# Attention and cosine router: state in four quarters of the array, narrow matmuls on column tiles, counts by a scan, and a new order on each engine

## Chip, cores, metric

The kernel runs on one core of one Trainium2 chip. The metric is the device time of one execution in microseconds (us), median of several runs. All arithmetic is fp32.

## What is computed

An attention block with a decaying state (RWKV-5 form) feeds a top-1 router with eight experts. Cut to what matters:

```python
B, H, S, D = 4, 8, 768, 48            # attention
for t in range(S):
    cur = einsum('bhd,bhe->bhde', u * k_t, v_t)
    y[t] = einsum('bhd,bhde->bhe', r_t, state + cur)
    state = w * state + einsum('bhd,bhe->bhde', k_t, v_t)
x = y as (B*S, H*D) = (3072, 384)     # router, E = 8 experts, F = 1024
logits = unit(x) @ unit(expert_emb).T / tau
e = argmax(logits); gate = softmax(logits)[e]
out = gate * (relu(x @ w1[e]) @ w2[e])
```

The kernel cuts the 768 steps into six chunks of C = 128. One **unit** is one chunk of one batch, for all eight heads, so there are 24 units, and the four units of one chunk are a **group**. Inside a chunk the scores between the 128 steps are a masked 128 x 128 matrix (`AT`), and what is older comes from the state. Heads are treated in NP = 4 pairs; a pair's 48-wide heads lie at partitions 0 to 47 and 64 to 111 (DP = 64, PP = 112).

## The kernel before

One unit's work goes through these functions (`own_rows`, `carry` and `logits` stand, as they were, in the removed lines of the diff further down). `mm` and `nc.tensor` are TensorE (PE), `nc.vector` is VectorE (DVE), `nc.scalar` is ScalarE (ACT), `nc.gpsimd` is GpSimd (POOL). The PSUM buffers (`k.ps`) are single, but for the tags "tp" and "at", which have two buffers each and are handed out in turn: `rt`, `kt` and `yrows` take "tp" one after the other.

```python
def turn(k, i):
    nc = k.nc
    R, Kw = k.loaded[i][1], k.Kpad[i % len(k.Kpad)]
    rt = k.ps.tile([128, NP, C], F32, name="rt", tag="tp")
    for p in range(NP):
        nc.tensor.transpose(rt[:, p, :], pair(R, p), k.ident)
    RT = k.work.tile([128, NP, C], F32, name="RT", tag="RT")
    nc.vector.tensor_mul(RT, rt, k.rpow)
    kt = k.ps.tile([128, NP, C], F32, name="kt", tag="tp")
    for p in range(NP):
        nc.tensor.transpose(kt[:, p, :], pair(Kw, p), k.ident)
    KT = k.work.tile([128, NP, C], F32, name="KT", tag="KT")
    nc.scalar.copy(KT, kt)
    k.RT[i], k.KT[i] = RT, KT

def scores(k, i):
    nc = k.nc
    RT, KT = k.RT[i], k.KT.pop(i)
    at = [k.ps.tile([128, NP, C], F32, name="at", tag="at") for _ in range(2)]
    for p in range(NP):
        for s in range(2):
            rows = slice(s * DP, s * DP + D)
            nc.tensor.matmul(at[s][:, p, :], KT[rows, p, :], RT[rows, p, :], start=True, stop=True)
    k.AT[i] = []
    for s in range(2):
        a = k.work.tile([128, NP, C], F32, name=f"AT{s}", tag=f"AT{s}")
        nc.vector.tensor_mul(a, at[s], k.umask[:, None, :].to_broadcast([128, NP, C]))
        k.AT[i].append(a)

def states(k, i):
    nc = k.nc
    c, b = divmod(i, B)
    if c == NCH - 1:
        return
    V, Kw = k.loaded[i][2], k.Kpad[i % len(k.Kpad)]
    st = k.ps.tile([128, NP, 2 * D], F32, name="st", tag="st")
    for p in range(NP):
        nc.tensor.matmul(st[0:PP, p, :], pair(Kw, p)[:, 0:PP], pair(V, p), start=True, stop=True)
    k.st[i] = st

def sums(k, i):
    nc = k.nc
    mm = nc.tensor.matmul
    c, b = divmod(i, B)
    V, RT, AT, T = k.loaded[i][2], k.RT.pop(i), k.AT.pop(i), k.state[b]
    y = k.ps.tile([128, NP, C], F32, name="y", tag="y")
    if c > 0:
        for p in range(NP):
            mm(y[0:PP, p, :], T[:, p, 0:PP], RT[:, p, :], start=(p == 0), stop=False, skip_group_check=True)
    for p in range(NP):
        for s in range(2):
            mm(
                y[s * DP : s * DP + D, p, :], V[:, 2 * p + s, :], AT[s][:, p, :],
                start=(c == 0 and p == 0), stop=True, skip_group_check=True,
            )
    yT = k.yT[i % len(k.yT)]
    if c > 0:
        nc.scalar.copy(yT[0:PP], y[0:PP])
    else:
        for s in range(2):
            heads = slice(s * DP, s * DP + D)
            nc.scalar.copy(yT[heads], y[heads])
    if b == 0:
        k.groups[c] = group(k, c)

def rows(k, i):
    nc = k.nc
    c, b = divmod(i, B)
    yT = k.yT[i % len(k.yT)]
    y = k.ps.tile([128, NP, 2, DP], F32, name="yrows", tag="tp")
    for p in range(NP):
        nc.tensor.transpose(
            y[:, p].rearrange("q s d -> q (s d)")[:, 0:PP], yT[0:PP, p, :], k.ident[0:PP, 0:PP]
        )
    X = k.groups[c].X[:, b, :].rearrange("q (p s d) -> q p s d", p=NP, s=2)
    nc.vector.tensor_add(X, y[:, :, :, 0:D], k.xd.pop(i).rearrange("q (p s) d -> q p s d", s=2))
    del k.loaded[i]

def turn_rows(k, g, b):
    nc = k.nc
    X = g.X[:, b, :]
    xp = k.ps.tile([128, NK, C], F32, name="xp", tag="xp")
    for m in range(NK):
        nc.tensor.transpose(xp[:, m, :], X[:, m * 128 : (m + 1) * 128], k.ident)
    g.xT[b] = k.work.tile([128, NK, C], F32, name="xT", tag="xT")
    nc.scalar.copy(g.xT[b], xp)

def ranks(k, g):
    mm = k.nc.tensor.matmul
    g.rank = k.ps.tile([128, B, E], F32, name="rank", tag="st")
    mm(g.rank, k.umask, g.oh, start=True, stop=False)
    for b in range(1, B):
        mm(g.rank[:, b:B, :], k.ones, g.oh[:, 0 : B - b, :], start=False, stop=False, skip_group_check=True)
    mm(g.rank, k.ones, k.cum[:, None, :].to_broadcast([128, B, E]), start=False, stop=True)

def taken(k, g):
    g.take = k.ps.tile([QS, 128], F32, name="take", tag="st")
    for b in range(B):
        k.nc.tensor.matmul(
            g.take, g.what[:, b].rearrange("p q s -> p (q s)"), g.lane[:, b, :], start=(b == 0), stop=(b == B - 1)
        )
```

The loop below issues the instructions in program order, and each engine runs its own in that order. `on(f, i)` calls f for unit i, `of_group` the same for a unit of an earlier group object, and `whole(f, i)` calls f for the group whose last unit is i, once in four rounds. Functions such as `choose` (the arg-max over the logits, six small DVE instructions), `gates` (softmax of the chosen expert), `places` (position of each token in its expert's list) and `listed` (one-hot rows for `taken`) work on one group.

```python
def attention(k):
    units = B * NCH
    def on(f, i):
        if 0 <= i < units:
            f(k, i)
    def of_group(f, i):
        if 0 <= i < units:
            f(k, k.groups[i // B], i % B)
    def whole(f, i):
        if 0 <= i < units and i % B == B - 1:
            f(k, k.groups[i // B])
    emb = build_experts(k)
    for i in range(-1, units + 7):
        j = i - SETTLED * B
        if 0 < i + AHEAD < units:
            load(k, i + AHEAD)
        if i < 2:
            next(emb)
        whole(summed, i - 6)
        whole(places, i - 4)
        on(own_rows, i)
        on(turn, i + 1)
        on(scaled, i + 2)
        on(own, i + 1)
        on(states, i)
        of_group(squares, i - 1)
        whole(choose, i - 3)
        whole(listed, i - 5)
        if j == 10:
            k.lists = turned_lists(k, perm, "st")
            lists = taken_by_rank(k, k.lists)
            first = [Early(k, r, *lists, w) for r, w in zip(LAST, k.weights)]
        on(sums, i)
        on(carry, i)
        on(scores, i + 1)
        on(rows, i)
        of_group(put, i)
        on(own_sum, i + 1)
        of_group(turn_rows, i - 1)
        of_group(logits, i - 2)
        whole(ranks, i - 3)
        whole(gates, i - 3)
        if i == units:
            first[0].hidden(0)
        whole(taken, i - 5)
        # ... (cut) j == 7, 8, 9, 10: after four chunks, the experts are ordered by load, and
        # two experts' weights and first token tiles are fetched
        if i == units + 1:
            first[0].hidden(1)
        if i == units + 2:
            first[0].rows(0)
        if i == units + 4:
            first[0].rows(1)
            # ... (cut) counts, out(to)
            first[1].hidden(0)
    # ... (cut) final order, gathers; then the eight expert blocks
```

`first[...]` are two "early" experts, whose work (`early_h`, `early_y`) fills TensorE while the last lists are made. After the loop, eight expert blocks follow; the change does not touch them.

Of the kernel before, what the change touches and what calls it, by code (L numbers as in the profile page):

```python
# [10 lines left out]
F32 = mybir.dt.float32  # L11
# [9 lines left out]
C = 128  # L21
NCH = S // C
DP = 64
# [89 lines left out]
def build_consts(k):  # L113
# [21 lines left out]
    k.yT = [k.aconst.tile([128, NP, C], F32, name=f"yT{i}") for i in range(2)]  # L135
    for t in k.yT:
        nc.gpsimd.memset(t, 0.0)
    for b in range(B):
        t = k.aconst.tile([128, NP, 2 * DP], F32, name=f"state{b}")
        nc.gpsimd.memset(t, 0.0)  # L140
        k.state.append(t)
# [9 lines left out]
    k.qt = numbers(k, "qt", [QS, QS], [[TM, 2], [0, E], [1, TM]], 0, 0)  # L151
    k.turned = numbers(k, "turned", [QS, QS], [[0, 2], [1, E], [0, TM]], 1, 0)
    k.part = pool.tile([QS, 1], I32, name="part")
# [9 lines left out]
    k.sums = pool.tile([QS, 128], F32, name="sums")  # L163
    nc.gpsimd.memset(k.sums, 0.0)

    k.cum = pool.tile([128, E], F32, name="cum")


def build_turned(k):
# [4 lines left out]
    bits = pool.tile([QS, 3], I32, name="bits")  # L174
    nc.vector.tensor_scalar(bits[:, 0:1], k.part, 2, E - 1, ALU.arith_shift_right, ALU.bitwise_and)
    nc.vector.tensor_scalar(bits[:, 1:2], k.part, 3, None, ALU.bitwise_and)
    nc.vector.tensor_scalar(bits[:, 2:3], k.part, 5, 2, ALU.arith_shift_right, ALU.arith_shift_left)
    own = pool.tile([QS, 3], F32, name="own")
    nc.vector.tensor_copy(own, bits)
    nc.vector.tensor_add(own[:, 1:2], own[:, 1:2], own[:, 2:3])  # L180
    k.mask = pool.tile([QS, E], F32, name="mask")
    nc.vector.tensor_scalar(k.mask, k.number[0:QS], own[:, 0:1], None, ALU.is_equal)
# [26 lines left out]
def build_experts(k):  # L209
# [16 lines left out]
    k.ent = k.const.tile([128, NK, E], F32, name="ent")  # L226
    nc.vector.tensor_copy(k.ent, ps)
# [74 lines left out]
def own_rows(k, i):  # L302
    xd = k.work.tile([128, H, D], F32, name="xd", tag="xd")
    diag, V = k.diag.pop(i), k.loaded[i][2]
    for h in range(H):
        k.nc.scalar.mul(xd[:, h, :], V[:, h, :], diag[:, h : h + 1])  # L306
    k.xd[i] = xd


def turn(k, i):  # L310

    nc = k.nc
    R, Kw = k.loaded[i][1], k.Kpad[i % len(k.Kpad)]
# [3 lines left out]
    RT = k.work.tile([128, NP, C], F32, name="RT", tag="RT")  # L317
    nc.vector.tensor_mul(RT, rt, k.rpow)
# [3 lines left out]
    KT = k.work.tile([128, NP, C], F32, name="KT", tag="KT")  # L322
    nc.scalar.copy(KT, kt)  # L323
    k.RT[i], k.KT[i] = RT, KT

# [16 lines left out]
# [4 lines that stand above are left out]
    if c == NCH - 1:  # L346
        return
    V, Kw = k.loaded[i][2], k.Kpad[i % len(k.Kpad)]
    st = k.ps.tile([128, NP, 2 * D], F32, name="st", tag="st")
    for p in range(NP):  # L350
        nc.tensor.matmul(st[0:PP, p, :], pair(Kw, p)[:, 0:PP], pair(V, p), start=True, stop=True)
    k.st[i] = st


def carry(k, i):
# [5 lines left out]
    for s in range(2):  # L361
        rows = slice(s * DP, s * DP + D)
        part = T[rows, :, s * DP : s * DP + D]
        nc.vector.tensor_add(part, part, st[rows, :, s * D : (s + 1) * D])  # L364
    for s in range(2):
        rows = slice(s * DP, s * DP + D)
        part = T[rows, :, s * DP : s * DP + D]
        nc.gpsimd.tensor_mul(part, part, k.wC[rows])  # L368


def sums(k, i):

# [5 lines left out]
    y = k.ps.tile([128, NP, C], F32, name="y", tag="y")  # L378
    if c > 0:
        for p in range(NP):  # L380
            mm(y[0:PP, p, :], T[:, p, 0:PP], RT[:, p, :], start=(p == 0), stop=False, skip_group_check=True)
    for p in range(NP):
        for s in range(2):
            mm(  # L384
                y[s * DP : s * DP + D, p, :], V[:, 2 * p + s, :], AT[s][:, p, :],
                start=(c == 0 and p == 0), stop=True, skip_group_check=True,
            )
    yT = k.yT[i % len(k.yT)]
    if c > 0:
        nc.scalar.copy(yT[0:PP], y[0:PP])  # L390
    else:
        for s in range(2):
# [1023 lines left out]
```

## Time and profile before

The time is 457.1 us (median of 3 runs, 456.83 to 458.7). The profiled execution spans 458.0 us.

| stretch of the profiled execution | us | PE busy | DVE busy | ACT busy | POOL busy |
|---|---|---|---|---|---|
| start up to the `at` of unit 4 | 38.11 | 31.71 | 20.92 | 18.60 | 25.95 |
| units of chunk 1 | 27.07 | 26.30 | 17.97 | 16.90 | 19.16 |
| units of chunk 2 | 27.69 | 27.36 | 18.18 | 15.97 | 19.98 |
| units of chunk 3 | 27.68 | 27.35 | 17.83 | 15.97 | 18.36 |
| units of chunk 4 | 27.68 | 27.35 | 17.82 | 15.97 | 18.34 |
| chunk 5 up to the `at` of the last unit | 19.50 | 18.27 | 14.30 | 11.63 | 9.82 |
| last unit and lists, up to the first expert block | 40.62 | 38.26 | 14.19 | 8.19 | 12.92 |
| expert blocks to the end | 249.65 | 233.28 | 135.90 | 70.83 | 53.87 |

Each row is one window of the trace; an edge between rows is the start of the `at` matmuls of a unit (38.11, 65.18, 92.87, 120.55, 148.23 and 167.73 us after the span's start), and the last one is 208.35 us, the first transpose of the first expert block. Busy is the time in which the engine had an instruction running. Matmuls are pipelined, so a busy PE need not be one that works at its peak: one fp32 matmul is recorded as two instructions of some 270 ns each, while the next one may start 109 ns later. A transpose is one such record.

Lines such as L334 are lines of the kernel before; a line of the timeline gives start, duration, engine, line, operation, what is written and what is read, the number of instructions merged into it, and in brackets how long the engine had been idle and what released it.

### The profile page before, as it was taken

The page shows a single profiled execution, that of the slowest core. Times are in us where ns is not written, and L with a number is a line of the kernel's source. Part 1 is how long each engine was busy: PE and PEld are TensorE (multiplying, and loading weights), DVE is VectorE, ACT ScalarE, POOL GpSimd, SP SyncE. Part 2 cuts the span into 40 slices and gives each one's busy share as a digit, 9 for nine tenths or more (in the row PEclk, how much of TensorE's full clock was granted, in tenths as well). Part 3 has the DMA queues.
Part 4 walks back from the last instruction along what each step waited for, and adds up shares of the span by engine and source line. Part 5 has one row for each costly group of instructions (what it writes and reads, how often), then busy time and mean ns, then how long its engine had stood idle before and what let it go on. Part 6 is the DMA issues. An engine that isn't in the chain of part 4 may idle for free. (4 is left out here: it accounts for less than half of the span.)

```text
span 458.0 us, 8806 instructions
## 1 busy us (share of the span) xinstructions
PE 429.9 (94%) x3266; PEld 391.2 (85%) x3266; DVE 257.1 (56%) x611; ACT 174.0 (38%) x497; POOL 178.4 (39%) x260
## 2 busy tenths in 40 slices
PE   8879999999999998999999999999999999999970
PEld 3668989889888888777899999999999999899660
DVE  4556865765756773325676685715726636565310
ACT  2377646656556643113233323323323224132110
POOL 7765676685675732144004114113113113200310
PEclk9999999999999997999999999999999999999995
DMA  8766546546453188022435362433443351040110
GB/s 176 153 140 141 114 94 140 122 89 138 99 111 87 36 309 330 0 69 88 140 140 183 122 211 69 148 109 127 140 162 90 147 173 53 34 156 1 51 39 20
DMA packets 93799, 54.36 MB, mean 119 GB/s; under 512 B 76937, under 2 KB 88380, under 8 KB 93746
## 3 DMA queue, kind: packets, MB, share of 16 engines
q1 hardware_dynamic: 89024, 43.85, 34.7%
q0 software_dynamic: 3296, 9.44, 6.2%
q8 instruction: 28, 0.46, 0.4%
q10 hardware_dynamic: 1426, 0.41, 0.4%
q14 instruction: 25, 0.20, 0.1%
HBM read 44.45 MB, written 9.63 MB: 118 GB/s over the span
## 5 line engine op out<-in xcount | busy, mean ns | idle before, releaser
L1157 POOL DMA_INDIRECT out_dram<-y,to x25 | 30.5, 1220 | 179.7 <-issue 91.8
L1033 PE MATMUL ps<-xTe,w 128*128 128x192 f32 (+3 forms) x336 | 62.9, 327 | 0.0
L1033 PEld LDWEIGHTS ps<-xTe,w 128*128 128x128 f32 x336 | 55.9, 190 | 0.5
L306 ACT ACTIVATE xd<-V,diag 128x48 f32<-128x48 f32 x192 | 45.8, 321 | 19.3 <-DVE diag L298 14.9
L338 DVE TENSOR_TENSOR AT<-at,umask 128x512 f32<-128x512 f32 x48 | 30.9, 686 | 34.2 <-PE at L334 34.2
L1040 ACT ACTIVATE hT<-hT 128x384 f32<-128x384 f32 (+3 forms) x42 | 22.0, 523 | 33.8 <-DVE hT L1063 21.1
L1097 PE MATMUL ps<-Tw,Sh 128*128 128x192 f32 x192 | 32.5, 326 | 0.0
L334 PE MATMUL at<-RT,KT 48*128 48x128 f32 x384 | 27.9, 285 | 4.4 <-ACT KT L323 3.4
L1097 PEld LDWEIGHTS ps<-Tw,Sh 128*128 128x128 f32 x192 | 31.4, 190 | 0.0
L368 POOL TENSOR_TENSOR state<-state,wpow 48x192 f32<-48x192 f32 x40 | 20.4, 510 | 28.2 <-DVE state L364 26.7
L334 PEld LDWEIGHTS at<-RT,KT 48*128 48x128 f32 x384 | 23.3, 187 | 9.3 <-ACT KT L323 5.1
L899 POOL DMA_INDIRECT G<-xs,take x25 | 26.4, 1056 | 9.0 <-issue 5.2
L1033 PE MATMUL ps<-Tx,Sw 128*128 128x192 f32 (+3 forms) x168 | 29.7, 326 | 0.0
L1033 PEld LDWEIGHTS ps<-Tx,Sw 128*128 128x128 f32 x168 | 27.6, 190 | 0.1
L384 PE MATMUL y<-AT,V 128*48 128x128 f32 x384 | 25.9, 277 | 0.0
L1050 DVE TENSOR_TENSOR u<-ps,p 128x384 f32<-128x384 f32 (+3 forms) x14 | 7.8, 557 | 31.7 <-PE ps L1033 30.9
L292 POOL TENSOR_TENSOR KU<-KU,Rpad 128x384 f32<-128x384 f32 x24 | 24.0, 1001 | 1.9
L283 POOL TENSOR_TENSOR Kpad<-K,kpow 128x384 f32<-128x384 f32 x23 | 23.0, 1000 | 3.0 <-DVE kpow L101 1.8
L291 POOL TENSOR_TENSOR KU<-K,u_bc 128x384 f32<-128x384 f32 x24 | 24.0, 1000 | 0.3 <-DVE diag L298 0.3
L490 ACT COPY xT<-xp 128x384 f32<-128x384 f32 x24 | 11.5, 479 | 31.8 <-PE xp L488 31.8
L1097 PE MATMUL ps<-w,hT 128*128 128x192 f32 x128 | 23.4, 326 | 0.0
L384 PEld LDWEIGHTS y<-AT,V 128*48 128x48 f32 x384 | 19.8, 122 | 3.0
(234 smaller groups left out, 903.1 us busy)
## 6 DMA issues: line engine op xcount, KB each, us to landing
w<-in_moe_w_dram SPq DMA_DIRECT2D x16, 1536.0 KB, 6.6
K<-in_k_dram SPq DMA_DIRECT2D x24, 192.0 KB, 3.5
V<-in_v_dram SPq DMA_DIRECT2D x24, 192.0 KB, 3.6
xs<-X SPq DMA_DIRECT2D x24, 192.0 KB, 2.0
Rpad<-in_r_dram SPq DMA_DIRECT2D x23, 192.0 KB, 3.8
G<-xs,take POOLq DMA_INDIRECT x27
out_dram<-y,to POOLq DMA_INDIRECT x25
Rpad<-in_r_dram ACTq DMA_DIRECT2D x1, 192.0 KB, 3.9
```

The source lines that it names most:

```text
L283: k.nc.gpsimd.tensor_mul(k.Kpad[i % len(k.Kpad)][:, :, 0:D], k.loaded[i][0], k.kpow)
L291: nc.gpsimd.tensor_mul(KU, K, k.u_bc)
L292: nc.gpsimd.tensor_mul(KU, KU, R[:, :, 0:D])
L306: k.nc.scalar.mul(xd[:, h, :], V[:, h, :], diag[:, h : h + 1])
L334: nc.tensor.matmul(at[s][:, p, :], KT[rows, p, :], RT[rows, p, :], start=True, stop=True)
L338: nc.vector.tensor_mul(a, at[s], k.umask[:, None, :].to_broadcast([128, NP, C]))
L384: mm(y[s * DP : s * DP + D, p, :], V[:, 2 * p + s, :], AT[s][:, p, :], start=(c == 0 and p == 0), stop=True, skip_group_check=True,)
L899: nc.gpsimd.indirect_dma_start(out=G[0:n, :], out_offset=None, in_=k.xs[:, :], in_offset=IndirectOffsetOnAxis(ap=take[0:n], axis=0), bound ...
L1033: nc.tensor.matmul(ps[:, j, :], weights[:, (f + j) * 128 : (f + j + 1) * 128], moving, start=(first and j == 0), stop=True, skip_group_che ...
L1040: nc.scalar.activation(h, h, ACT.Relu)
L1097: nc.tensor.matmul(ps, a[:, f, :], b[:, f, :], start=(first and f == 0), stop=(f == NF // 2 - 1), skip_group_check=True)
L1157: k.nc.gpsimd.indirect_dma_start(out=k.out[:, :], out_offset=IndirectOffsetOnAxis(ap=k.to[0:here, j : j + 1], axis=0), in_=y[0:here, :], i ...
```

## The change

The change has these parts:

- **State in quarters.** The state of a pair was a 112 x 112 block whose two off-diagonal blocks are zero, and one matmul with K = 128 multiplied it. Now each head's 48 x 48 state is its own matmul in one quarter (64 x 64) of the array; four of them, in four quarters, can run side by side. The result goes to two PSUM banks, one for each row half, so tag "y" has two buffers, and the logits lose theirs.
- **State without empty blocks.** The new contribution `st` is made by head, with 64 columns of weights and 48 moving columns, instead of by pair with 112 and 96. So `carry` adds and scales all heads in one instruction each, where there were two each.
- **Logits on column tiles.** One token tile's logits were 3 matmuls with 128 columns of weights and 8 moving columns. Now the weights are the expert embeddings padded to 32 columns, the tokens move, and the four units of a group stand on four column tiles of 32; a copy and a transpose turn the result.
- **Slices on column tiles.** `taken` puts even and odd units on two column tiles of 64.
- **Counts by a scan.** The count of tokens of each expert in earlier units came from three matmuls with a matrix of ones and four GpSimd additions. Now a DVE scan sums the units, and one matmul remains.
- **Order.** `turn` is split in two; `own_rows` in two halves around `KT` and `squares`; `own` is done one unit earlier; `own_sum` now stands ahead of `carry`; the softmax pieces (`norms`, `exps`, `gates`) and the list pieces are spread over later rounds.

The diff, cut to its core (comments in the text mark the cuts; setup of constants, `turner` and the unchanged tail are left out):

```diff
+    k.ent = k.const.tile([128, NK, 32], F32, name="ent")
+    nc.vector.memset(k.ent, 0.0)
+    nc.vector.tensor_copy(k.ent[:, :, 0:E], ps)
# ...
-def own_rows(k, i):
-    xd = k.work.tile([128, H, D], F32, name="xd", tag="xd")
-    diag, V = k.diag.pop(i), k.loaded[i][2]
-    for h in range(H):
-        k.nc.scalar.mul(xd[:, h, :], V[:, h, :], diag[:, h : h + 1])
-    k.xd[i] = xd
+def own_rows(k, i, half):
+    if half == 0:
+        k.xd[i] = k.work.tile([128, H, D], F32, name="xd", tag="xd")
+    diag, V = k.diag[i], k.loaded[i][2]
+    for h in range(half * H // 2, (half + 1) * H // 2):
+        k.nc.scalar.mul(k.xd[i][:, h, :], V[:, h, :], diag[:, h : h + 1])
# ...
-    st = k.ps.tile([128, NP, 2 * D], F32, name="st", tag="st")
+    st = k.ps.tile([128, NP, D], F32, name="st", tag="st")
     for p in range(NP):
-        nc.tensor.matmul(st[0:PP, p, :], pair(Kw, p)[:, 0:PP], pair(V, p), start=True, stop=True)
+        for s in range(2):
+            h = 2 * p + s
+            nc.tensor.matmul(
+                st[s * DP : (s + 1) * DP, p, :], Kw[:, h, :], V[:, h, :], start=True, stop=True, skip_group_check=True
# ...
-    for s in range(2):
-        rows = slice(s * DP, s * DP + D)
-        part = T[rows, :, s * DP : s * DP + D]
-        nc.vector.tensor_add(part, part, st[rows, :, s * D : (s + 1) * D])
-    for s in range(2):
-        rows = slice(s * DP, s * DP + D)
-        part = T[rows, :, s * DP : s * DP + D]
-        nc.gpsimd.tensor_mul(part, part, k.wC[rows])
+    part = T[:, :, 0:D]
+    nc.vector.tensor_add(part, part, st)
+    nc.gpsimd.tensor_mul(part, part, k.wC)
# ...
-    y = k.ps.tile([128, NP, C], F32, name="y", tag="y")
-    if c > 0:
-        for p in range(NP):
-            mm(y[0:PP, p, :], T[:, p, 0:PP], RT[:, p, :], start=(p == 0), stop=False, skip_group_check=True)
-    for p in range(NP):
-        for s in range(2):
-            mm(
-                y[s * DP : s * DP + D, p, :], V[:, 2 * p + s, :], AT[s][:, p, :],
-                start=(c == 0 and p == 0), stop=True, skip_group_check=True,
-            )
-    yT = k.yT[i % len(k.yT)]
-    if c > 0:
-        nc.scalar.copy(yT[0:PP], y[0:PP])
-    else:
-        for s in range(2):
-            heads = slice(s * DP, s * DP + D)
-            nc.scalar.copy(yT[heads], y[heads])
+    y = [k.ps.tile([128, NP // 2, C], F32, name="y", tag="y") for _ in range(2)]
+    for q in range(NP // 2):
+        for u in range(2) if c > 0 else ():
+            for s in range(2):
+                mm(
+                    y[s][u * DP : (u + 1) * DP, q, :], T[s * DP : s * DP + D, 2 * q + u, :],
+                    RT[s * DP : s * DP + D, 2 * q + u, :], start=(q == 0), stop=False, skip_group_check=True,
+                )
+    for s in range(2):
+        for q in range(NP // 2):
+            for u in range(2):
+                p = 2 * q + u
+                mm(
+                    y[s][u * DP : u * DP + D, q, :], V[:, 2 * p + s, :], AT[s][:, p, :],
+                    start=(c == 0 and q == 0), stop=True, skip_group_check=True,
+                )
+        yT = k.yT[i % len(k.yT)]
+        if c > 0:
+            nc.scalar.copy(yT[0:PP, s], y[s][0:PP])
+        else:
+            for u in range(2):
+                heads = slice(u * DP, u * DP + D)
+                nc.scalar.copy(yT[heads, s], y[s][heads])
# ...
-    y = k.ps.tile([128, NP, 2, DP], F32, name="yrows", tag="tp")
-    for p in range(NP):
-        nc.tensor.transpose(
-            y[:, p].rearrange("q s d -> q (s d)")[:, 0:PP], yT[0:PP, p, :], k.ident[0:PP, 0:PP]
-        )
-    X = k.groups[c].X[:, b, :].rearrange("q (p s d) -> q p s d", p=NP, s=2)
-    nc.vector.tensor_add(X, y[:, :, :, 0:D], k.xd.pop(i).rearrange("q (p s) d -> q p s d", s=2))
-    del k.loaded[i]
+    y = k.ps.tile([128, 2, NP // 2, 2 * DP], F32, name="yrows", tag="tp")
+    for s in range(2):
+        for q in range(NP // 2):
+            nc.tensor.transpose(y[:, s, q, 0:PP], yT[0:PP, s, q, :], k.ident[0:PP, 0:PP])
+    def by_bank(t):
+        return t.rearrange("t (g s) d -> t s g d", s=2)
+    X = k.groups[c].X[:, b, :].rearrange("t (h d) -> t h d", d=D)
+    nc.vector.tensor_add(
+        by_bank(X), y.rearrange("t s q (u d) -> t s (q u) d", d=DP)[:, :, :, 0:D], by_bank(k.xd.pop(i))
+    )
+    del k.loaded[i], k.diag[i]
# ...
-def logits(k, g, b):
-    xT = g.xT.pop(b)
-    if b == 0:
-        g.lg = k.ps.tile([128, B, E], F32, name="lg", tag="lg")
+def logits(k, g):
+    mm = k.nc.tensor.matmul
+    lgT = k.ps.tile([128, 128], F32, name="lgT", tag="st")
     for m in range(NK):
-        k.nc.tensor.matmul(g.lg[:, b, :], xT[:, m, :], k.ent[:, m, :], start=(m == 0), stop=(m == NK - 1))
+        for b in range(B):
+            mm(
+                lgT[b * 32 : (b + 1) * 32, :], k.ent[:, m, :], g.xT[b][:, m, :],
+                start=(m == 0), stop=(m == NK - 1), tile_position=(0, b * 32), skip_group_check=True,
+            )
+    g.lgT = lgT
+def logits_out(k, g):
+    t = k.rt.tile([128, 128], F32, name="lgT", tag="lgT")
+    k.nc.scalar.copy(t, g.lgT)
+    g.lgT = t
+def turn_logits(k, g):
+    lg = k.ps.tile([128, B, 32], F32, name="lg", tag="xp")
+    k.nc.tensor.transpose(lg.rearrange("q b e -> q (b e)"), g.lgT, k.ident)
+    g.lg = lg[:, :, 0:E]
# ...
+    g.seq = p.tile([128, E, B + 1], F32, name="seq", tag="seq")
+    g.oh = g.seq[:, :, 1 : B + 1]
# ...
+def before(k, g):
+    nc = k.nc
+    nc.vector.tensor_copy(g.seq[:, :, 0], k.cum)
+    run = k.rt.tile([128, E, B + 1], F32, name="run", tag="run")
+    nc.vector.tensor_tensor_scan(
+        run.rearrange("p e b -> p (e b)"), k.fresh.rearrange("p e b -> p (e b)"), g.seq.rearrange("p e b -> p (e b)"),
+        0.0, ALU.mult, ALU.add,
+    )
+    nc.vector.tensor_copy(k.cum, run[:, :, B])
+    g.pre = run[:, :, 0:B]
 def ranks(k, g):
     mm = k.nc.tensor.matmul
-    g.rank = k.ps.tile([128, B, E], F32, name="rank", tag="st")
+    g.rank = k.ps.tile([128, E, B], F32, name="rank", tag="st")
     mm(g.rank, k.umask, g.oh, start=True, stop=False)
-    for b in range(1, B):
-        mm(g.rank[:, b:B, :], k.ones, g.oh[:, 0 : B - b, :], start=False, stop=False, skip_group_check=True)
-    mm(g.rank, k.ones, k.cum[:, None, :].to_broadcast([128, B, E]), start=False, stop=True)
-def gates(k, g):
+    mm(g.rank, k.ones, g.pre, start=False, stop=True)
# ...
-    for b in range(B):
-        nc.gpsimd.tensor_add(k.cum, k.cum, g.oh[:, b, :])   # in places
# ...
-    g.take = k.ps.tile([QS, 128], F32, name="take", tag="st")
+    g.take = k.ps.tile([2 * QS, 128], F32, name="take", tag="st")
     for b in range(B):
         k.nc.tensor.matmul(
-            g.take, g.what[:, b].rearrange("p q s -> p (q s)"), g.lane[:, b, :], start=(b == 0), stop=(b == B - 1)
+            g.take[b % 2 * QS : (b % 2 + 1) * QS], g.what[:, b].rearrange("p q s -> p (q s)"), g.lane[:, b, :],
+            start=(b < 2), stop=(b >= B - 2), skip_group_check=True,
# ...
+        whole(logits_out, i - 3)
+        on(turn_r, i + 1)
+        on(own_rows, i, 0)
+        on(turn_k, i + 1)
+        whole(turn_logits, i - 3)
         on(scaled, i + 2)
-        on(own, i + 1)
+        for n in (0, 1) if i < 0 else (i + 2,):
+            on(own, n)
         on(states, i)
         of_group(squares, i - 1)
+        on(own_rows, i, 1)
+        whole(norms, i - 2)
         whole(choose, i - 3)
+        whole(before, i - 3)
+        whole(exps, i - 4)
+        whole(located, i - 4)
+        whole(gates, i - 5)
         whole(listed, i - 5)
+        on(own_sum, i + 1)
         if j == 10:
             k.lists = turned_lists(k, perm, "st")
             lists = taken_by_rank(k, k.lists)
         on(scores, i + 1)
         on(rows, i)
         of_group(put, i)
-        on(own_sum, i + 1)
         of_group(turn_rows, i - 1)
-        of_group(logits, i - 2)
+        whole(logits, i - 2)
# ...
-        whole(gates, i - 3)
# ...
-        return self.pool.tile(shape, dtype, name=name, tag=tag, bufs={"tp": 2, "at": 2}.get(tag, 1))
+        return self.pool.tile(shape, dtype, name=name, tag=tag, bufs={"tp": 2, "at": 2, "y": 2}.get(tag, 1))
```

## Prediction, made before the changed kernel ran

> **What bounds the kernel now.** I read three views in this order: the windows (the table above), the timeline of one unit, and the waits of TensorE. The windows say that in chunks 2 to 4 PE is busy for 27.35 of 27.68 us, DVE for 17.8, ACT for 16, POOL for 18 to 20. Chunk after chunk costs the same 27.7 us, and the four chunks from 38.11 to 148.23 take 110.1 us. In the expert blocks PE is busy for 233.28 of 249.65 us, and the change does not touch them. So the change can only act on the first 208 us. The timeline of one unit, from one `at` to the next, is this (PE alone):
>
> ```profile
> 106.42 1.16 PE L334 MATMUL at<-RT,KT 48*128 48x128 f32 x16
> 107.51 0.60 PE L406 MATMUL yrows<-ident,yT 112*128 112x112 f32 x4
> 107.95 0.49 PE L488 MATMUL xp<-ident,X 128*128 128x128 f32 x3
> 108.28 0.73 PE L503 MATMUL lg<-ent,xT 128*128 128x8 f32 x6
> 108.87 0.64 PE L316 MATMUL rt<-ident,Rpad 128*128 128x128 f32 x4
> 109.52 0.63 PE L321 MATMUL kt<-ident,Kpad 128*128 128x128 f32 x4
> 109.98 0.94 PE L351 MATMUL st<-V,Kpad 128*112 128x96 f32 x8
> 110.75 1.05 PE L381 MATMUL y<-RT,state 128*112 128x128 f32 x8
> 111.73 1.08 PE L384 MATMUL y<-AT,V 128*48 128x128 f32 x16
> 112.74 1.16 PE L334 MATMUL at<-RT,KT 48*128 48x128 f32 x16
> ```
>
> and DVE in the same time:
>
> ```profile
> 107.61 1.29 DVE L338 TENSOR_TENSOR AT<-at,umask 128x512 f32<-128x512 f32 x2 [1.36 <-PE at L334]
> 108.82 0.55 DVE L410 TENSOR_TENSOR X<-yrows,xd 128x384 f32<-128x384 f32 x1
> 109.28 0.54 DVE L298 TENSOR_REDUCE diag<-KU 128x8 f32<-128x384 f32 x1
> 109.74 0.68 DVE L318 TENSOR_TENSOR RT<-rt,rpow 128x512 f32<-128x512 f32 x1
> ```
>
> Read the starts, not the durations. The differences of the starts are what each step costs PE: `at` 1.09, `yrows` 0.44, `xp` 0.33, `lg` 0.59, `rt` 0.65, `kt` 0.46, `st` 0.77, state 0.98, `AT` 1.01; together 6.32 us. One of them is too long: `rt` and `kt` are four transposes each, and `rt` takes 0.65 where `kt` takes 0.46. `kt` needs the "tp" buffer that `yrows` had, and that is free when DVE's `X` is done, at 108.82 + 0.55 = 109.37. The first weights of `kt` are loaded at 109.48. So although PE looks full, in such a unit it already waits some 0.2 us for DVE. **This is the point on which my number turns.** From the start of `at` to that of `kt` are 3.10 us (106.42 to 109.52), set by a chain across two engines: `at` 1.09, a short latency, two `AT` masks at 0.6 each, `X` 0.55.
>
> The other waits of PE between 13 and 208 us are small:
>
> ```profile
> PE at L334 <- ACT KT L323: 3.4, 5, 1.5
> PE yrows L406 <- ACT yT L390: 1.6, 1, 1.6
> PE yrows L406 <- ACT yT L394: 1.3, 3, 0.4
> PE st L351 <- DVE at L548: 1.3, 4, 0.3
> ```
>
> The first and the third of these lie in chunk 0, the second in the last unit.
>
> **What the Trainium skill says.** (1) "TensorE: Matmul & The Clock Gate", section "The mechanism" (packing small matmuls): matmuls at different tile positions run concurrently, with starts some 4 ns apart. The trace agrees: the 16 records of `y<-AT,V` come in pairs that start 6 to 7 ns apart, a pair each 109 ns, as on two column tiles. (2) "TensorEngine Tiling (Array Packing)", section "Key Properties": a change of tiling mode drains the array. The trace shows it: from the last state matmul to the first `AT` matmul, from there to `at` and from `at` to `yrows` the starts are 203, 203 and 202 ns apart, where 98 to 109 is usual. So I take 0.1 us for each switch. (3) Same page as (1), section "LDWEIGHTS (loading the stationary operand)": loading takes time by the columns alone. `lg`, with 8 moving columns and 128 of weights, steps at 112 ns; `st`, with 112 of weights, at 98. Both agree with 0.875 ns per column of fp32 weights, which gives 56 ns for 64 columns. (4) The same page, Part 1 on the clock gate: an idle array drops to half its clock. The mean granted clock in the last row before the expert blocks is 0.92, and 1.00 in the rows before it.
>
> **The change, part by part.** First what PE would need in a unit.
> - `st`: 8 matmuls, 16 records, on two column tiles: 8 pairs x 56 ns = 0.45, and 0.1 for a switch of mode: 0.55 (was 0.77).
> - State: 16 records in four quarters: 4 x 109 ns = 0.44, and a switch and a start of 0.13: 0.57 (was 0.98).
> - `AT` keeps 1.01 and `at` 1.09, `yrows` with its switch 0.54.
> - Logits: 4 x 0.59 = 2.36 us of a group become 24 records on four column tiles: 6 x 109 = 0.65, two switches 0.2: 0.85 in one unit of the group, and a transpose of 0.11.
> - Ranks: 10 records of 112 ns become 4: 1.12 to 0.45. Slices: 8 records of 127 ns become 4 pairs and two switches: 1.02 to 0.7.
>
> By PE alone a plain unit is then 1.09 + 0.54 + 0.33 + 0.44 + 0.46 + 0.55 + 0.57 + 1.01 = 4.99 us, a group 4 x 4.99 + 0.85 + 0.11 + 0.45 + 0.7 = 22.1.
>
> But PE will not be alone. With `lg` gone, `kt` could start 1.09 + 0.54 + 0.33 + 0.44 = 2.40 us after `at`; DVE's `AT`, `AT`, `X` keep it until 3.10. So 0.7 us of each plain unit becomes a wait of `kt` for `X`, and a plain unit is 3.10 + 0.46 + 0.55 + 0.57 + 1.01 = 5.69. Where a group's logits (0.85), ranks or slices stand ahead of `rt`, they fill that gap, and cost little or nothing: the unit with the logits is 5.69 + (2.40 + 0.85 - 3.10) = 5.84, the one with the ranks and the turned logits 5.80. A group is 2 x 5.69 + 5.84 + 5.80 = 23.0 us. That DVE has `diag` ahead of `carry` now, and `X` straight before the next `RT`, does not shorten this chain.
>
> ACT: `xT` 0.48, eight `xd` 1.91, `KT` 0.56, `squares` 0.73, and `yT`, one copy of 0.58, now two of some 0.36 each (my estimate for half the elements): 4.4 us in 5.7. But `yT` stands behind the second half of `xd`, and `yrows` needs it 1.09 us after `at` starts. I put xT at 2.2 us after `at`; with the rows above in order `yT` ends 6.6 us after it, and `yrows` comes at 5.69 + 1.09 = 6.78. So it just holds in a plain unit, and I add 0.4 us a group for those with a copy of the logits or an exponential more. A further 0.4 is kept for starts and switches that I do not see: 23.8 for 27.5 (110.1 / 4) today. **Four groups save 4 x 3.7 = 14.8 us.** POOL loses one of two `carry` products (0.51) and the four additions, DVE one of two additions (0.35); neither is on the path.
>
> The start up to 38.11: there the waits are `at` on `KT` (up to 1.5) and `yrows` on two `yT` copies of 0.56. `diag` comes earlier, `KT` goes between the halves of `xd`, and half of the `yT` copies can start while PE is still at `AT`. Units 1 to 3, today 5.9 to 6.0 us each, come to 5.2 to 5.5, unit 1 gains about 1.4: **3.2 saved.** Units 20 to 23 (19.5 us): no `st` or only small things to save, and 12 small DVE instructions that order the experts delay `RT` as before: **1.5 saved.**
>
> The last stretch (40.62 us): PE is busy with early expert work, and this work stays. Saved: the logits of three units ahead of the first `early_h` 1.4, ranks 0.6, slices 0.6. Added: the turned logits stand straight ahead of `ranks`, and between the two lie six instructions of `choose` (1.2) and three of `before` (0.7) with latencies, so PE waits 2.5 us which today lie beneath `early_h`. Then `places`, `exps`, `gates`, `listed` and POOL's `what` come to about 4.1 us after the ranks, beneath an `early_y` of 2.9: 1.2 more. **Net 1.1 us lost.**
>
> Sum: 14.8 + 3.2 + 1.5 - 1.1 = 18.4; 457.1 - 18.4 = 438.7; I say 438.
>
> **The rivals.** *PE stays the bound and gains in full.* For it: PE is the busiest engine by far, and the waits of the page are small. Against it: `rt` at 0.65. It makes 27.5 - 22.1 = 5.4 a group, and some 431 us. *DVE's chain is all, and narrow matmuls do not get cheap.* If 16 narrow records cannot be issued in 0.45 us, `st` and the state stay at 0.9 each; then a unit is 3.10 + 0.46 + 0.9 + 0.9 + 1.01 = 6.4 and the group 26: about 450. For it: nothing in this trace has more than two matmuls side by side; against it: both pairs start 6 ns apart. *ACT becomes the bound* through `yT`: each 0.3 us by which it is late costs 0.3 x 20 = 6 us, so 444. *The lists' chain at the end* exposes more than I think, and an idle PE gets half its clock once more: 4 to 6 us, 443.
>
> **Range and chances.** The middle two cases (438 and 443) seem likeliest to me, the full gain has perhaps one chance in seven, hardly any gain one in ten. So 429 to 448 in 8 of 10. The limit of 2% is 448.0: faster 0.89, the same 0.10, slower 0.01.
>
> **What would show it.** In the timeline of the changed kernel `kt` starts 3.1 us after `at` in plain units, released by `X`; units come at 5.7 us; four state matmuls start within some 20 ns; `lgT` takes under 1 us; at the end ranks wait some 2.5 us for DVE. Wrong would be: plain units near 5.0 (the wait for `X` does not bind), or above 6.2 (narrow matmuls are dear), or `yrows` that waits for `yT` by more than 0.2, or a second stretch at half clock.

## The result, and the profile after

The changed kernel takes 440.28 us (median; 439.26 to 440.58, four runs) against 457.9 us for the kernel before in the same comparison: a ratio of 0.961, with a 95% interval of 0.957 to 0.965. The prediction was 438 us, with a range of 429 to 448.

The stretches of the profiled executions, with the same edges as in the table of the kernel before (the `at` matmuls of units 4, 20 and 23, and the first expert block):

| stretch, us | before | predicted saving | after | saved |
|---|---|---|---|---|
| start to unit 4 | 38.11 | 3.2 | 35.43 | 2.7 |
| chunks 1 to 4 | 110.12 | 14.8 | 94.89 | 15.2 |
| chunk 5 to the last `at` | 19.50 | 1.5 | 17.08 | 2.4 |
| last unit and lists | 40.62 | -1.1 | 41.40 | -0.8 |
| expert blocks | 249.65 | 0 | 249.59 | 0.1 |
| sum | 458.0 | 18.4 | 438.4 | 19.6 |

The profiled execution of the kernel before was timed at 460.14 us, above its median, so the traces differ by 2 us more than the medians do (17.6). The caution on the clock, below the table of the experiments, says where that comes from.

The timeline of TensorE (PE) in a plain unit, that is one without logits, ranks or slices, to be held against the one in the prediction:

```profile
83.11 1.16 PE L344 MATMUL at<-RT,KT 48*128 48x128 f32 x16
84.20 0.60 PE L423 MATMUL yrows<-ident,yT 112*128 112x112 f32 x4
84.64 0.49 PE L509 MATMUL xp<-ident,X 128*128 128x128 f32 x3
84.97 0.60 PE L321 MATMUL rt<-ident,Rpad 128*128 128x128 f32 x4
86.20 0.63 PE L332 MATMUL kt<-ident,Kpad 128*128 128x128 f32 x4 [0.63 <-DVE X L429]
86.76 0.67 PE L363 MATMUL st<-V,Kpad 128*64 128x48 f32 x16
87.36 0.67 PE L392 MATMUL y<-RT,state 48*64 48x128 f32 x16
87.95 1.08 PE L400 MATMUL y<-AT,V 128*48 128x128 f32 x16
88.97 1.16 PE L344 MATMUL at<-RT,KT 48*128 48x128 f32 x16
```

and that of VectorE (DVE) in the same time:

```profile
84.30 1.29 DVE L348 TENSOR_TENSOR AT<-at,umask 128x512 f32<-128x512 f32 x2 [1.35 <-PE at L344]
85.50 0.55 DVE L429 TENSOR_TENSOR X<-yrows,xd 128x384 f32<-128x384 f32 x1
85.97 0.68 DVE L323 TENSOR_TENSOR RT<-rt,rpow 128x512 f32<-128x512 f32 x1
```

`st` and the state matmuls now cost 0.60 us each (0.77 and 0.98 before). `lg` is gone from the unit, and in its place stands a gap: `rt` is over after 0.44 us, but `kt` starts only 1.23 us after `rt`, and the bracket says that PE was idle for 0.63 us of that until `X`. `X` ends at 85.50 + 0.55 = 86.05. The bracket counts from the end of the last transpose; counted by the starts, `kt` comes 1.23 - 0.44 = 0.79 us later than it could. From `at` to `kt` are 3.09 us, as before (3.10).

The unit that has the logits, 6.09 us long, holds their matmuls (`lgT`) and the transpose that turns them (`lg`):

```profile
96.72 0.86 PE L525 MATMUL lgT<-xT,ent 128*32 128x128 f32 x24
97.51 0.66 PE L321 MATMUL rt<-ident,Rpad 128*128 128x128 f32 x4
98.01 0.60 PE L332 MATMUL kt<-ident,Kpad 128*128 128x128 f32 x4
98.44 0.27 PE L540 MATMUL lg<-ident,lgT 128*128 128x128 f32 x1
98.65 0.67 PE L363 MATMUL st<-V,Kpad 128*64 128x48 f32 x16
```

The windows show the same from afar (columns: us, then busy time of PE, its weight loads, DVE, ACT, POOL, with the number of instructions; granted clock; DMA share; GB/s). The first row is one group, the second the last stretch:

```profile
59.50:83.11 23.61, 22.75 (x356) 18.79 (x354) 16.76 (x46) 16.23 (x60) 16.87 (x24) 1.00 0.65 136
147.41:188.81 41.40, 34.01 (x254) 26.65 (x252) 14.88 (x68) 8.48 (x28) 9.96 (x12) 0.92 0.45 159
```

PE idles 0.86 us in each group, which are the 0.63 of the plain unit and 0.23 in the unit that has the ranks. In the last stretch PE is busy for 34.0 us of 41.4, where it was 38.3 of 40.6: the work became less by 4.2 us, and the waits grew from 2.4 to 7.4. The largest waits of PE there (total us, times, longest; `early_x` are the transposes of the token rows that were gathered for the early experts):

```profile
PE early_x L910 <- DMA G<-xs,take: 1.9, 2, 1.4
PE rank L578 <- DVE seq L556: 1.3, 1, 1.3
PE yrows L423 <- ACT yT L406: 1.3, 1, 1.3
PE take L658 <- POOL what L643: 1.0, 1, 1.0
PE lg L540 <- ACT lgT L534: 0.8, 1, 0.8
```

Before, this stretch had two waits, 1.6 us of `yrows` for `yT` and 0.7 at its end; the latter is still there.

### The profile page after: what moved, and what is told of

It is laid out like the page before. It is cut to its first block, busy times and chain, and to the rows that moved or that the text cites. A ratio compares the mean times of both kernels' runs of the same rounds, so it can differ in the third digit from the quotient of the medians.

```text
span 438.4 us, 9319 instructions
## 1 busy us (share of the span) xinstructions
PE 404.5 (92%) x3556; PEld 357.2 (81%) x3556; DVE 251.0 (57%) x610; ACT 176.6 (40%) x531; POOL 161.4 (37%) x218
## 4 chain that ended last, share of the span: by engine, by line
PE 77%; DVE 7%; POOL 4%; ACT 4%; issue 3%; DMA 2%; POOLq 0%; DVEq 0%; ACTq 0%
PE ps L1107 22%; PE ps L1171 16%; PE ps L1211 5%; PE at L344 4%; PE ps L1224 4%; PE y L400 3%; PE early_h L920 3%; PE wake L67 3%; DVE AT L348 2%; PE ps L1085 2%; PE ps L1055 2%; PE kt L332 2%; PE early_y L931 2%; PE y L392 2%; PE st L363 2%
## 5 line engine op out<-in xcount | busy, mean ns | idle before, releaser
L312 ACT ACTIVATE xd<-V,diag 128x48 f32<-128x48 f32 x192 | 48.3, 325 | 0.2 <-DVE diag L303 0.2
L344 PEld LDWEIGHTS at<-RT,KT 48*128 48x128 f32 x384 | 23.3, 187 | 6.6 <-ACT xd L312 2.8
L1171 PEld LDWEIGHTS ps<-w,hT 128*128 128x128 f32 x128 | 21.3, 190 | 0.3
```

What stands on the lines that cost most here:

```text
L312: k.nc.scalar.mul(k.xd[i][:, h, :], V[:, h, :], diag[:, h : h + 1])
L1171: nc.tensor.matmul(ps, a[:, f, :], b[:, f, :], start=(first and f == 0), stop=(f == NF // 2 - 1), skip_group_check=True)
```

## The experiments

Two theories stood against each other for the units: a chain across two engines (`at`, two masks, `X`, and the "tp" buffer that `kt` needs) ends the gain, or TensorE's own work does. Two more questions were how much the new order does by itself, and what the last stretch lost. Times are medians; the ratio is to the kernel before, with its 95% interval. The stretches are those of one profiled execution of each kernel. No run separates the narrow matmuls (state, `st`, logits, ranks, slices) from each other; what each is worth is read from the traces alone.

| kernel | time, us | ratio | start | chunks 1-4 | chunk 5 | last | clock in last |
|---|---|---|---|---|---|---|---|
| before | 457.9 | | 38.11 | 110.12 | 19.50 | 40.62 | 0.92 |
| after | 440.28 | 0.961 (0.957 to 0.965) | 35.43 | 94.89 | 17.08 | 41.40 | 0.92 |
| e1 rows in "y" | 433.0 | 0.946 (0.942 to 0.949) | 34.64 | 89.72 | 16.57 | 40.82 | 0.96 |
| e2 old order | 446.85 | 0.978 (0.972 to 0.984) | 37.91 | 95.50 | 19.40 | 39.98 | 0.91 |
| e3 order alone | 452.4 | 0.990 (0.985 to 0.994) | 35.13 | 108.04 | 18.09 | 37.56 | 1.00 |
| e4 state first | 438.35 | 0.957 (0.954 to 0.960) | 34.74 | 92.73 | 17.08 | 42.07 | 0.92 |
| e5 `xp` twice | 444.38, one run | | 35.41 | 97.47 | 17.43 | 42.49 | 0.92 |
| e6 tail | 437.47 | 0.955 (0.951 to 0.958) | 34.30 | 94.90 | 17.09 | 38.50 | 0.96 |
| e7 weights | 438.15 | 0.956 (0.952 to 0.960) | 34.68 | 94.90 | 17.07 | 40.42 | 0.96 |
| e8 all four | 426.33 | 0.930 (0.926 to 0.934) | 34.42 | 88.20 | 16.58 | 36.55 | 1.00 |
| e9 weights later | 426.62 | 0.932 (0.928 to 0.935) | 34.32 | 88.19 | 16.57 | 35.77 | 1.00 |

Two cautions. The first is the clock. In the last stretch TensorE ran at half its clock for 6.8 us in the profiled executions of before, after and e4, for 3.4 in e1, e6 and e7, twice for 3.4 in e2 and e5, and not at all in e3, e8 and e9. Half the clock for 6.8 us costs up to 3.4 us. The medians hold this too: of eleven executions of the kernel before, five took 458.7 to 460.1 us at a mean clock of 0.979 or 0.980 over the whole, and six took 456.0 to 457.8 at 0.986 to 0.989. All four of the changed kernel ran at 0.979 to 0.983; held against the five at nearly that clock, it saves some 19 us, close to the 19.6 of the traces. The second is the start: the first `at` begins between 14.1 and 15.3 us in these kernels, so from the first column about 1 us can be chance.

**e1: `yrows` in a buffer of tag "y".**

```diff
-    y = k.ps.tile([128, 2, NP // 2, 2 * DP], F32, name="yrows", tag="tp")
+    y = k.ps.tile([128, 2, NP // 2, 2 * DP], F32, name="yrows", tag="y")
```

> One edit to the changed kernel: yrows takes a PSUM buffer of tag y and no longer one of tag tp, so kt needs not wait until DVE has read yrows. Theory (the chain at, AT, AT, X on DVE and the tp buffer hold kt back 0.63 us in a plain unit and 0.23 us in the unit with the ranks): kt follows rt at once, the plain unit falls from 5.86 to about 5.25 us, a group from 23.6 to about 22.8, the whole by 4 to 5 us to about 436. Rival (TensorE's own work is the bound already, and the wait is only the form that its slack takes): no change, 440. Second rival (ScalarE is next): the wait moves to yrows on yT and under 2 us are gained.

Measured: 433.0 us, 7.3 below the changed kernel. The timeline of PE in a plain unit, and the window of a group:

```profile
81.54 0.60 PE L321 MATMUL rt<-ident,Rpad 128*128 128x128 f32 x4
81.98 0.60 PE L332 MATMUL kt<-ident,Kpad 128*128 128x128 f32 x4
```

```profile
79.68:102.02 22.34, 22.34 (x355) 18.84 (x354) 16.75 (x48) 15.91 (x60) 15.47 (x20) 1.00 0.67 141
```

`kt` follows `rt` after 0.44 us, the plain unit takes 5.04 us and the group 22.34 us. PE is busy in all of it: it is the bound again, close to the 22.1 us that the prediction had worked out for "PE alone". The gain is larger than I had expected, since I had taken off only the 0.63 us of the bracket (5.86 to 5.25). By the starts `kt` came 0.79 us too late, and in the unit with the ranks 0.40 (0.87 for 0.47); these units are now 0.82 and 0.42 shorter. The theory of the chain holds, its size was too small, and both rivals fall. One word in the source gives a third of what the whole change took from a group (27.5 to 23.6).

**e5: more work beneath the wait.**

```diff
-    for m in range(NK):
-        nc.tensor.transpose(xp[:, m, :], X[...], k.ident)
+    for _ in range(2):
+        for m in range(NK):
+            nc.tensor.transpose(xp[:, m, :], X[...], k.ident)
```

> The changed kernel with the three xp transposes of each unit done twice: 0.33 us more work for TensorE, of the same result, ahead of rt. Theory (kt waits for DVE in a plain unit): the plain unit stays at 5.86 us and the one with the ranks grows by 0.1, since the work lies beneath the wait; the units with the logits (6.09) and the slices (5.80) have no such wait and grow by 0.3; four chunks come to 94.9 + 4 x 0.75 = 98 us. Rival (TensorE's work is the bound): every unit grows by 0.33 us, four chunks come to 100.2 us.

Measured: four chunks take 97.47 us. The plain unit stays at 5.86 us. So does the one with the ranks, which I had expected to grow by 0.1: its wait, 0.40 us by the starts, covers the added work too. The others go from 6.09 to 6.42 and from 5.80 to 6.11. The timeline of the plain unit:

```profile
85.92 0.82 PE L510 MATMUL xp<-ident,X 128*128 128x128 f32 x6
86.57 0.60 PE L321 MATMUL rt<-ident,Rpad 128*128 128x128 f32 x4
87.48 0.63 PE L332 MATMUL kt<-ident,Kpad 128*128 128x128 f32 x4 [0.30 <-DVE X L429]
```

The wait shrinks from 0.63 to 0.30 us, by just the work that was put in. So up to the size of the wait, work for PE ahead of `kt` is free in the plain unit. That less work there would save nothing follows from the same wait, but was not tried.

**e4: the state ahead of `st`.**

```diff
-        on(states, i)                      # in the loop, ahead of sums
+    states(k, i)                           # in sums, between the state matmuls and the AT ones
```

> One edit to the changed kernel: on TensorE the state matmuls (quarters) go ahead of st (two column tiles), so st and AT stand in one tiling mode and a unit has one change of mode less. If each change costs the 0.1 us that I put into the sum: 0.1 us less in each of the 16 units of chunks 1 to 4, 1.5 to 2 us less in all, about 438.5. Rival (the change of mode is hidden beneath the wait of kt, or costs nothing where no drain is seen): within 0.5 us of the changed kernel.

Measured: 438.35 us, 1.9 below the changed kernel, and 2.2 less in the four chunks; every unit is 0.13 to 0.14 shorter. The timeline:

```profile
84.99 0.67 PE L392 MATMUL y<-RT,state 48*64 48x128 f32 x16
85.59 0.67 PE L363 MATMUL st<-V,Kpad 128*64 128x48 f32 x16
86.09 1.04 PE L401 MATMUL y<-AT,V 128*48 128x128 f32 x16
87.07 1.16 PE L344 MATMUL at<-RT,KT 48*128 48x128 f32 x16
```

`st`, in the tiling mode of the `AT` matmuls that follow it, takes 0.50 instead of 0.60 us, and `AT` 0.98 instead of 1.01. These steps stand after the wait for `X`, so they count in full.

**e2: the old order with the narrow matmuls.**

```diff
-        on(turn_r, i + 1)
-        on(own_rows, i, 0)
-        on(turn_k, i + 1)
+        on(own_rows, i, 0)
+        on(own_rows, i, 1)
+        on(turn_r, i + 1)
+        on(turn_k, i + 1)
# and: no own_rows(i, 1) after squares, own(i + 1) in place of own(i + 2), own_sum(i + 1) after put in place of ahead of carry
```

> The changed kernel with the old order of own, own_rows (in one piece, ahead of the transposes), and own_sum (after X). The narrow matmuls, the scan and the logits stay. As predicted (the order matters at the start alone, and for ScalarE's yT within 0.1 us of time): 2 to 4 us slower than the changed kernel, 443. Rival (the order is what lets the narrow matmuls pay, since the old one puts xd behind diag, KT and yT behind xd): KT and yT come 0.3 to 0.8 us late in each unit, 8 to 18 us slower, 448 to 458, that is most of the gain gone.

Measured: 446.85 us (444.2 to 450.3). The four chunks lose only 0.6 us; the start loses 2.5 and chunk 5 2.3, in line with the first expectation, and the last stretch has the clock at 0.91. The median is 6.6 us above the changed kernel, where the trace accounts for 3.7. The rest goes with the clock: two of the four executions took 444.2 and 444.5 us at a mean clock of 0.981, near that of the changed kernel, and two took 449.2 and 450.3 at 0.971 and 0.969. At like clocks the order is thus worth about 4 us here. Why the rival fell shows in the timeline of a unit:

```profile
82.64 0.54 DVE L303 TENSOR_REDUCE diag<-KU 128x8 f32<-128x384 f32 x1
83.26 1.91 ACT L312 ACTIVATE xd<-V,diag 128x48 f32<-128x48 f32 x8 [0.95 <-DVE diag L303]
85.08 0.56 ACT L334 COPY KT<-kt 128x512 f32<-128x512 f32 x1
85.70 1.16 PE L344 MATMUL at<-RT,KT 48*128 48x128 f32 x16
```

ACT does stand idle for 0.95 us until `diag`, and `KT` ends at 85.64, just 0.06 us before `at`. So with the old order the chain through `diag`, `xd` and `KT` binds the unit, but at 5.92 us, and the one through `X` at 5.86: they are nearly equal. What the order is worth with `X` out of the way was not tried.

**e3: the new order alone**, on the kernel before (the same lines of the loop the other way round, all matmuls as they were).

> The kernel before with the new order of own, own_rows and own_sum alone; all matmuls as before. Theory (TensorE is the bound in chunks 1 to 4 of the kernel before, so order gives nothing there, only at the start where at waits for KT): 2 to 3 us faster than the kernel before, about 455. Rival (the order is the larger part of the gain): 447 or less.

Measured: 452.4 us (450.3 to 456.0), 5.4 below the kernel before, more than I had expected; at like clocks (0.986 to 0.989) it is 450.3 to 450.6 against 456.0 to 457.8, about 6.3, near the 6.5 that the traces show outside the last stretch. The start gives 3.0 us and chunk 5 1.4. The chunks give 2.1, 0.5 for each group: the unit with the ranks falls from 7.81 to 7.35 us. There `st` had waited 0.3 us (0.45 by the starts) for DVE's small `at` instruction, a wait that the prediction shows and did not charge. So the theory that the order gives nothing in the chunks is wrong by that much. The last stretch, at a clock of 1.00, is 3.1 us shorter, and that is what the half clock costs (0.08 of some 40 us); I don't put it down to the order.

**e6: the tail's `early_h` ahead of the ranks.**

```diff
-        if i == units + 1:
-            first[0].hidden(1)            # after the logits, ahead of their turning
+        if i == units + 2:
+            first[0].hidden(1)            # after the turned logits, ahead of ranks
```

> One edit to the changed kernel: the second half of the first early_h goes between the turned logits and the ranks of the last group, and no longer ahead of the turned logits. Theory (what the last stretch lost is the chain lgT, lg, choose, rank, exposed for 0.84 and 1.30 us): the wait of the ranks goes, some 0.6 us of wait of lg on ScalarE's copy stay, 1.5 us gained, about 438.7. Rival (the end is bound by the slices, which come from the ranks, so that moving them later under TensorE's work gives back what it gains): the wait of take grows by the same amount and nothing is gained.

Measured: 437.47 us, 2.8 below. The waits of PE in the last stretch are now:

```profile
PE early_x L910 <- DMA G<-xs,take: 2.2, 2, 1.4
PE yrows L423 <- ACT yT L406: 1.3, 1, 1.3
PE take L658 <- POOL what L643: 1.0, 1, 1.0
PE ps L1055 <- DVE earlyy L938: 0.7, 1, 0.7
PE lgT L525 <- DVE sums L665: 0.4, 1, 0.4
PE lg L540 <- ACT lgT L534: 0.4, 1, 0.4
```

The wait of the ranks (1.3) is gone, that of `lg` halved, and the one of `take` has not grown. That is 1.7 us less of waiting, of which `early_x` takes back 0.3 (1.9 to 2.2); the rest of the 2.9 us by which the last stretch is shorter goes with the clock, 0.96 instead of 0.92 (3.4 us less at half clock, 1.7 us). The theory holds; of the 2.8 us in the median, some 1.4 are shown to be its own.

**e7 and e9: the second expert's weights later.**

```diff
-            for w, r in zip(k.weights, LAST):      # j == 8
-                load_weights(k, expert_number(k, r), w)
+            load_weights(k, expert_number(k, LAST[0]), k.weights[0])
# ... (cut) further up in the loop, ahead of sums:
+        if j == 11:                                # e9: j == 12
+            load_weights(k, expert_number(k, LAST[1]), k.weights[1])
```

> One edit to the changed kernel: the weights of the second early expert are loaded three rounds later, after the gathers of the early experts' tokens have been issued. Theory (early_x waits 1.9 us for the gathered rows because they stand behind 6 MB of weights, and the faster units left them less time): the gather lands several us sooner, the wait goes, 1.5 to 1.9 us gained, about 438.5. Rival (yT on ScalarE, 1.3 us of wait just before, or the second expert's weights, then late, take its place): under 0.5 us gained.

Measured: 438.15 us, but `early_x` still waits 1.1 us for the gathered rows and 0.7 for the copy of the first of them. The loads were issued at 150.75 us, and the packets of the gather ran from 150.77 to 154.7: the edit had put the two side by side. The gather landed 8.0 us after the last `at`, where it was 8.4. So the 2.1 us below the changed kernel are not shown to come from it; the clock accounts for some 1.7, and the two executions at a mean clock of 0.979 and 0.981 took 440.9 and 439.2 us, as much as the changed kernel. In e9, on top of the other edits, the loads come one round later again:

> The four edits together, with the second expert's weights one round later again, behind the last unit's store of X. In the kernels with the weights three rounds later, these were issued in the same moment in which the packets of the gathered rows began, so they still shared the DMA engines, and early_x still waited 1.8 us. Theory (the gather shares the queues with the weights): alone on them, its packets take under 2 us instead of 3.9, the wait falls to under 0.5 us, and the whole by 1 to 1.5 us against the kernel with the four edits (426.3). Rival (issue and first packet set the landing): no change.

Measured: 426.62 us against 426.33 without. The timeline of PE:

```profile
145.99 0.55 PE L911 MATMUL early_x<-ident,G 128*128 128x128 f32 x3 [0.62 <-DMA G<-xs,take]
146.95 0.55 PE L911 MATMUL early_x<-ident,G 128*128 128x128 f32 x3 [0.41 <-DMA G<-xs,take]
```

The wait falls from 1.8 to 1.0 us and the last stretch by 0.8, yet the time does not show it. The packets of the gather took 3.1 us where it had been 4.1, not the under 2 that I had expected. So sharing the DMA engines with the weights made up about half of this wait; that moving them is worth anything in the time is not shown. What remains goes with the issue: 3.0 us pass from the first gather's issue (140.30) to its first packet (143.27). In the changed kernel, behind the weights of both experts, it was 4.6 us (148.62 to 153.26), and at its final lists, with no weights under way, 1.8 us (180.93 to 182.68); why was not tried.

**e8: rows in "y", state first, the tail and the weights together.**

> All four edits together: yrows in a buffer of tag y, state ahead of st, the tail's early_h moved, the second weights later. If they add up: 440.3 - 7.3 - 1.9 - 1.5 - 1.7 = 428. With yrows out of the way TensorE's own work is the bound, so the saved change of mode should count in every unit. Rival (ScalarE's yT holds units of under 5 us): four chunks stay at 89.7 us and the sum is about 430.

Measured: 426.33 us, ratio 0.930 (0.926 to 0.934), 3.2% below the changed kernel. The window of the four chunks:

```profile
34.42:122.62 88.20, 87.48 (x1405) 74.39 (x1405) 68.46 (x187) 64.21 (x238) 63.90 (x82) 1.00 0.68 144
```

PE is busy for 87.48 of 88.20 us, so TensorE and not ScalarE is the bound. The median falls by 14.0 us, about the sum of the four edits (7.3 + 1.9 + 2.8 + 2.1 = 14.1), but not all of this is their work: its six executions had mean clocks of 0.984 to 0.989, those of the changed kernel 0.979 to 0.983, and its last stretch none at half clock, which is worth up to 3.4 us. Whether the edits brought that about was not tried. Of the 2.2 us that e4 gave, 1.5 are there (89.72 to 88.20): three units of a group are 0.14 shorter, but the plain one is not (5.04 to 5.07). In it the state matmuls, now earlier, take 0.77 us instead of 0.60:

```profile
81.51 0.83 PE L392 MATMUL y<-RT,state 48*64 48x128 f32 x16
82.28 0.67 PE L363 MATMUL st<-V,Kpad 128*64 128x48 f32 x16
```

One of their two "y" buffers is that of `yrows`, and waits for `X`, which ends at 81.63; the record that the trace shows as released by `X` starts at 81.69. The wait has moved from `kt` to the state, at about a fifth of its size (0.17 us for 0.79).

## Why the prediction held, point by point

- **The chain at, AT, AT, X, kt.** Predicted 3.10 us from `at` to `kt` and 0.70 of waiting; measured 3.09 and, counted in the same way, 0.79. The prediction had 2.40 us of work ahead of `kt` where there are 2.30: it charged `yrows` 0.54 us, though the 1.09 us of `at` already hold that change of tiling mode, and `yrows` takes 0.44 as before. e1 and e5 show the chain from both sides. In the prediction it stood on one interval, `rt` taking 0.65 instead of 0.46 us.
- **The narrow matmuls.** `st` 0.55 predicted, 0.60 measured; state 0.57 and 0.60; logits 0.85 and 0.79. The unit with the logits takes 6.09 us instead of 5.84, above all because the logits are turned in that same unit, which costs 0.21 us to the next step; the prediction had put 0.11 for it in the unit with the ranks. The starts in the trace show 4 state records within 20 ns, the first such four followed by the next after 160 ns and then every 109 to 110, the pairs of `st` 58 ns apart (56 predicted), and 199 to 203 ns at most changes of mode. My plain unit was 0.17 too short because `kt` to `st` to state cost 1.16, not 1.01. The reserve of 0.4 in a group that I kept for this was too small, but the other 0.4, for ScalarE's `yT`, was not needed in chunks 1 to 4: a group came to 23.6 for 23.8. Here two errors cancelled, and that is luck. So is the PE time of a plain unit, 4.99 predicted and 5.04 in e1, where the `yrows` charged too high covers most of what `kt`, `st` and state were charged too low.
- **The order.** That it does not shorten the chain in plain units is right: 5.92 to 5.86 (e2). The start gained 2.7 for 3.2, and 3.2 when counted from the first `at` (23.3 to 20.2 us), 2.7 of it by the order alone (20.6 in e3). Unit 1 gained the 1.4 that I gave it (5.47 to 4.11). One sign of being wrong did come there, at little cost: `yrows` waits for `yT` by up to 0.37 us in chunk 0.
- **Chunk 5 was sized too small**: 1.5, measured 2.4. The order alone already gives 1.4 there (e3), and the old order takes 2.3 back (e2). I had let the DVE instructions that order the experts hide most of it. One of the waits of `at` for `KT` that the prediction placed in chunk 0, of 0.3 us, lies in this chunk.
- **The last stretch** came to the right sum by luck: 1.1 us lost in the prediction, 0.8 measured, but the work fell by 4.2 us and not by 2.6, and the waits grew by 5.0 and not by 3.7. By the starts, logits, ranks and slices saved 1.9, 1.1 and 0.8 us (1.4, 0.6 and 0.6 predicted), and the state, not in the sum, 0.4. The ranks waited 1.3 us where 2.5 was predicted; `lg`, ahead of them, 0.8, which was not predicted; `take` 1.0 (1.2). Missed altogether: `early_x` waits 1.9 us for the gathered rows. Before, the gather landed 7.2 us after the last `at` and `early_x` began at 8.6. Now it is issued later with respect to the last `at` and lands at 8.4, while PE has done its work ahead of `early_x` after 6.3.
- **The rivals.** PE as the bound at 22.1 us a group was right for e1 (22.3) and wrong for this kernel; narrow matmuls too dear to issue, and ScalarE as the bound, both fell. (The 450 us given for the former is some 2.5 above its own sum: four groups of 26 leave 447.5.) A second stretch at half clock did not come in the profiled execution.

## What to carry to other kernels

Before counting a saving on the busiest engine, walk the loop once by the starts of its instructions and ask which buffer each step needs and when its last reader is done: the chain through other engines that today makes a step 0.2 us late made it 0.8 us late once the engine was faster. When such a wait appears, another buffer for the step can be a cheap cure, as with `yrows`, and what is then saved on the busy engine ahead of that step can count in full. Instructions that were hidden under work of the busiest engine come to light when that work is cut; here it was so at the end of the phase, where the waits grew from 2.4 to 7.4 us.

## What the runs showed of the hardware

- Fp32 matmuls in four quarters run side by side: the records of the state matmuls start in fours, 6 to 7 ns apart, and the next four come 109 ns later (160 after the first four), where one record at a time on the whole array also took 109 ns (state before the change).
- A change of tiling mode adds some 0.09 us between two starts, whatever the pace: 203 ns from `kt` to `st`, from `AT` to `at` and from `at` to `yrows`, and 199 from the state to `AT`, where 103 to 109 is usual, and 151 from `st` to the state, where 58 is usual. One change less was worth 0.13 to 0.14 us in each unit (e4).
- The same stretch of the program had TensorE at half clock for 6.8 us, 3.4 us, twice 3.4 us, or not at all (0.92 before, 1.00 in e3, whose waits in that stretch are alike), and executions of one kernel differ in it. That it comes from idle time, as the prediction took it, is not shown: the longest single wait of PE there was 1.6 us before and 1.8 in e3. What decides it was not tried and stays open.
